# Block-sparse attention with a feed-forward layer: neighbour blocks of two tiles copied in v's own order, and conversions and keys moved

## The chip, the cores and the metric

The kernel runs on one core of a Trainium2 chip. The core has a matrix engine (TensorE, PE in the profile; its weight loads are PEld), a vector engine (VectorE, DVE), an activation engine (ScalarE, ACT), a general engine (GpSimd, POOL) and an engine that mainly issues DMAs (SyncE, SP). Each takes its own instructions in order; semaphores connect them. SBUF is the on-chip memory of 128 partitions, PSUM the accumulator memory that PE writes to. The metric is the device time of one execution in microseconds, as the median of several runs.

## The reference

Attention over a sparse set of blocks, then a feed-forward layer with a squared ReLU, all in float32. q, k and v are (4 batches, 8 heads, 768 positions, 64). Positions form 24 blocks of 32.

```python
mask = np.abs(blk_i - blk_j) <= window          # window = 1: a block and its two neighbours
mask = mask | (blk_i == 0) | (blk_j == 0) | (blk_i == n_blocks - 1) | (blk_j == n_blocks - 1)
for qb in range(n_blocks):
    for kb in sampled_blocks[qb]:               # 3 sampled blocks for each block of queries
        mask[qb * block:(qb + 1) * block, kb * block:(kb + 1) * block] = True
scores = np.where(mask, scores, -1000000000.0)
...
attn = attn / (np.sum(attn, axis=-1, keepdims=True) + 1e-09)
return np.matmul(attn, v)
...
h = np.maximum(x @ w_in, 0.0)                   # x: (3072, 512), w_in: (512, 2048)
return h * h @ w_out                            # w_out: (2048, 512)
```

So a block of queries sees eight blocks of keys: the first and the last of the sequence, three sampled ones and its own neighbourhood of three. The softmax doesn't depend on the order of these eight, as long as scores and values use the same one. The first and the last block of queries see all 24.

## The kernel before

**Tiles and stages.** The 768 positions of a batch are six tiles of 128 (four blocks each), 24 tiles in all, in the list `order`; index `k` counts them from 0. Three tiles (`UC`) make a chunk, whose 384 positions go through the feed-forward layer together. A stage of the program runs the feed-forward layer of one chunk (`moe(c)`) beside the attention of the next one. The start, before the first `moe(0)`, is the attention of tiles 0 to 2 alone, together with the first and last query blocks of batch 0 (`Whole`, four of them, tiles `g`, `pg`, `ptg`, `pTg`, `pvg` in the profile). Each tile's attention is two halves of four heads (`Half`): scores on PE (line 373, tile `s`), maxima on DVE (385), exponentials on ACT (432, `p`), transposes on PE (447, `pt`), their copies to SBUF on ACT (457, `pT`), products with the values on PE (471, `pv`), and the division by the sum on DVE (487 to 495).

**Order.** The order of each engine's instructions is written out by hand. A `Stream` counts steps (`now`). In the start a new unit begins every 5 steps, the wholes at 0 to 15 and the halves at 20 to 45, and each unit's next part comes so many steps later as `LAG_0` says (scores, +2 maxima, +2 exponentials, +3 transposes, +2 copies, +2 values, +2 norm). Between the steps the loop at line 951 hands out one copy from the list `fixed` to ACT (from step 7), one from `moves` to DVE (from step 22), one piece of the lists in `later` (keys) to POOL every second step, and one call of `cut_next` at each step that `CUT_0` names.

**Values of a tile.** A tile's eight blocks of values lie in two buffers, `V[k][0]` and `V[k][1]`, each of 128 partitions, that is four slots of 32, for two half-widths `i` and four query blocks `j`. `V[k][0]` holds the first and last block (slots 0, 1) and sampled blocks 0 and 1. `V[k][1]` holds sampled block 2 in slot 0 and the three neighbours in slots 1 to 3. For tiles 1 and 2 the neighbours aren't fetched from HBM: `copy_window` (211) copies each of them, 32 partitions by 260 elements, from `vn`, which has all of v of the batch with block b in partitions (b mod 4)·32 and column block b // 4. That is 12 copies for a tile and a half-width, 48 in all: 24 on ACT (`fixed`), 12 on POOL (ahead of the third tile's keys) and 12 on DVE (`moves`). The sampled blocks are fetched by SP (`load_sampled`, 303, issues on line 314), 65 KB each, with indices read into registers (`sampled`, 232).

**Keys of a tile.** `KG` holds first, last and sampled keys of a tile; POOL copies them from `kn` (`copy_keys`, 257; lines 267 and 288). The neighbours' keys are read straight from `kn`. So a half's scores are two pieces for each query block: one over three neighbouring blocks of `kn`, one over five blocks of `kg`. Keys of tiles 3 and 4 are appended to `later` as tiles 0 and 1 pass; two buffers alternate, so that tile 3 uses tile 0's, and tile 4 tile 1's.

**Weights.** The feed-forward weights come as 64-bit numbers and are converted to float32 by a pipeline that `cut_next` (768) pushes on by one: weight n is loaded by a DMA on POOL's queue (724), five calls later ACT does two operations (`cut`, 740 and 742), one call later DVE two (`cut_bits`, 751 and 752), one call later ACT and POOL split it where needed (758, 759). The order is four pieces of w_in, the first of w_out (`WO[0]`), and then both in turn. In `moe(0)` a call comes every 3 steps, and `need` (777) makes calls until a weight that is wanted has passed all stages. `moe(0)` runs over `f` from 0 to 15: `hidden` (line 820, `ph`; then ACT 824 and 827 make `gp`), and from f = 2 `project(f-2)` (line 848, `po`), which reads `gp` and `WO`. At f = 1 `split_wo` calls `need` for `WO[0]`. SINGLE pieces of w_in are split into two parts just ahead of their use (784 on ACT, 787 on POOL, `wi`).

Of the kernel before, what the change touches and what calls it, by code (L numbers as in the profile page):

```python
# [48 lines left out]
UC = 3  # L49
# [26 lines left out]
CUT_0 = (30, 5)  # L76
# [6 lines left out]
ON_ACT = 12  # L83
# [13 lines left out]
def tile_block_sparse_attention_moe(ctx: ExitStack, tc, kd, knd, qd, qgd, vd, vnd, samp, const, wcat, out):  # L97
# [113 lines left out]
    def copy_window(k, i, j, n, copy):  # L211

        b, t = order[k]
        blk = centre(NJ * t + j) - 1 + n
        assert 0 < blk < NBLK - 1
        r = blk % NJ * BLK
        copy(V[k][1][(1 + n) * BLK : (2 + n) * BLK, i, j], st["vn", b, i][r : r + BLK, blk // NJ])  # L217
# [85 lines left out]
    def load_sampled(k, u, eng, on):  # L303
        us = halves(k, u)
        if us is None:
            return
        b, t = order[k]
        VA, VB = values_of(k)
        vals = sampled(t, 1, on)
        v4 = columns(vd[b], us).rearrange("(a p) u c -> p a u c", p=BLK)  # L310
        for j in sorted(groups(t)):
            for r in range(NRAND):
                dst = VB[0:BLK, us, j] if r == 2 else VA[(2 + r) * BLK : (3 + r) * BLK, us, j]
                eng.dma_start(dst.unsqueeze(1), v4[:, bass.ds(vals[NRAND * j + r], 1)])  # L314
# [6 lines left out]
    class Half:  # L321
# [36 lines left out]
        def scores(self):  # L358
            b, t, u = self.b, self.t, self.u
            q, kg, kn = st["q", b, t], st["kg", b, t], st["kn", b, u]  # L360
            self.sb = [bank(f"s{self.name}_{e}") for e in range(2)]
            for i in range(2):
                pr = 2 * u + i
                for piece in range(2):
                    for g, j in enumerate(self.js):
                        c = centre(NJ * t + j)
                        for e in range(2):
                            r = slice(e * D, (e + 1) * D)
                            if piece == 0:
                                k, a, z = kn[r, c - 1 : c + 2, i, :], S_WIN, NSLOT  # L370
                            else:
                                k, a, z = kg[r, j, :, pr, :], 0, S_WIN
                            nc.tensor.matmul(  # L373
                                self.sb[e][g * BLK : (g + 1) * BLK, i * NSLOT + a : i * NSLOT + z],
                                q[r, j, pr, :],
                                k,
                                start=True,
                                stop=True,
                            )

# [535 lines left out]
    for k in range(1, UC):  # L916
# [11 lines left out]
    load_sampled(1, 0, nc.sync, SP)  # L928
    load_q(0, 2, own=begin)
    load_sampled(2, 1, nc.sync, SP)  # L930
    windows = {
        (k, u): [(copy_window, k, u, j, n) for j in range(NJ) for n in range(3)] for k in range(1, UC) for u in range(2)
    }
    for k in range(2):
        deque(copy_keys(0, k), 0)
    for _ in range(AHEAD):
        cut_next()
    for k in range(1, UC):
        if k == 1:
            for f, *at in windows[k, 0]:  # L940
                f(*at, nc.gpsimd.tensor_copy)
            deque(copy_keys(0, 2, begin), 0)
    fixed = [(copy_static, k, i) for k in range(UC) for i in range(2)]
    fixed += windows[2, 0] + windows[2, 1][:ON_ACT]
    moves = windows[1, 1] + windows[2, 1][ON_ACT:]
# [4 lines left out]
    now = 0  # L950
    while work.todo or work.running:
        work.step(now)
        now += 1
        if now % KEYS_N == 0 and later and next(later[0], True):
            later.pop(0)
# [3 lines left out]
        if now >= MOVES_0 and moves:  # L959
            f, *at = moves.pop(0)  # L960
            f(*at, nc.vector.tensor_copy)
        if now >= CUT_0[0] and (now - CUT_0[0]) % CUT_0[1] == 0:
            cut_next()
# [78 lines left out]
```

## Time and profile before

| what | us |
|---|---|
| median of 3 timed runs (lowest, highest) | 752.19 (750.61, 753.6) |
| the profiled execution: device time | 748.36 |
| its span, from the program's first instruction to its last | 746.6 |
| first `ph` matmul of `moe(0)` | 58.08 |

The profile page gives busy time by engine and by groups of instructions; `128x512 f32<-128x512 f32` is output and input in partitions by elements. Views by stretch and in order of time are read from the same execution, with times in us from the start of its span. A number in brackets with an arrow, as in `[0.49 <-PE pv L471]`, is how long the engine stood idle before an instruction, and what ended that. SPq is SP's queue, whose rows are the issues of DMAs, not their transfers.

### The profile page before, as it was taken

To read this page: it belongs to the slowest core of one execution; us is meant where nothing else is said; L and a number is where in the kernel's file an instruction comes from. 1 tells how busy PE (TensorE), PEld (TensorE's weight loads), DVE (VectorE), ACT (ScalarE), POOL (GpSimd) and SP (SyncE) were. 2 spreads that over 40 slices of the span, in tenths; PEclk is the share of its full clock that TensorE was granted. 3 is DMA by queue.
4 is the path that set the end of the run, shared out by engine and by line. 5 is a ranking of instruction groups with operands and counts; after the bars stand their busy time and mean duration, and the time that the engine had idled before them with its cause. 6 is when DMAs were issued, how large, how long until landed. Compare 5 with 4: busy or idle time off the path is not lost.

```text
span 746.6 us, 24386 instructions
## 1 busy us (share of the span) xinstructions
PE 717.3 (96%) x9000; PEld 596.6 (80%) x9000; DVE 509.1 (68%) x1052; ACT 518.5 (69%) x1145; POOL 497.0 (67%) x624
## 2 busy tenths in 40 slices
PE   4689999999999999999999999999999999999997
PEld 2566676668888888887888888887788888898996
DVE  5886886758885757667876665667878666555342
ACT  4996787888876866588786677578976776623222
POOL 6953644237876675767778567675777576877885
PEclk9999999999999999999999999999999999999999
DMA  8784889553533435543543445544344342101001
GB/s 274 227 234 144 242 258 338 134 151 78 144 93 91 139 92 162 151 106 91 143 86 99 120 99 158 162 98 129 84 128 107 90 126 54 34 1 43 0 2 43
DMA packets 85755, 92.44 MB, mean 124 GB/s; under 512 B 13539, under 2 KB 73444, under 8 KB 85636
## 3 DMA queue, kind: packets, MB, share of 16 engines
q1 hardware_dynamic: 79684, 68.03, 34.5%
q0 software_dynamic: 5664, 22.45, 9.0%
q8 instruction: 72, 1.18, 0.7%
q14 instruction: 47, 0.39, 0.2%
q10 hardware_dynamic: 288, 0.39, 0.1%
HBM read 84.53 MB, written 6.29 MB: 122 GB/s over the span
## 4 chain that ended last, share of the span: by engine, by line
PE 79%; ACT 8%; DMA 4%; DVE 3%; POOL 2%; issue 2%; SPq 1%; ACTq 0%; POOLq 0%; DVEq 0%
PE ph L820 32%; PE po L858 29%; PE s L373 6%; PE pv L471 5%; PE po L848 3%; DMA V<-in_v_dram 2%; ACT pm L418 2%; PE pvg L636 1%; ACT V L217 1%; DMA KG<-in_k_dram 1%; PE g L566 1%; PE xt L805 1%; ACT pg L591 1%; PE pt L447 1%; SPq L314 1%
## 5 line engine op out<-in xcount | busy, mean ns | idle before, releaser
L820 PE MATMUL ph<-xh,wi 128*128 128x384 f32 x832 | 238.1, 347 | 0.0
L418 ACT ACTIVATE pm<-p 32x256 f32<-32x256 f32 x528 | 219.1, 415 | 17.4 <-DVE p L393 9.9
L858 PE MATMUL po<-wo,gh 128*128 128x512 f32 x672 | 211.5, 396 | 0.0
L787 POOL TENSOR_TENSOR wi<-W,wi 128x512 fp32r<-128x512 f32 x104 | 142.8, 1373 | 71.3 <-DVE wi L786 37.5
L824 ACT ACTIVATE r<-ph 128x384 f32<-128x384 f32 x128 | 63.0, 493 | 167.9 <-PE ph L820 166.8
L787 POOL TENSOR_TENSOR wo<-WO,wo 128x512 fp32r<-128x512 f32 x112 | 144.7, 1292 | 50.1 <-DVE wo L786 42.1
L838 POOL TENSOR_TENSOR gl<-gf,gh 128x384 fp32r<-128x384 f32 x112 | 117.3, 1047 | 83.3 <-DVE gf L836 70.0
L820 PEld LDWEIGHTS ph<-xh,wi 128*128 128x128 f32 x832 | 150.6, 188 | 13.1 <-issue 6.2
L836 DVE SCALAR_TENSOR_TENSOR gf<-ph,r 128x384 f32<-128x384 f32 x112 | 62.3, 556 | 139.1 <-ACT r L824 119.4
L858 PEld LDWEIGHTS po<-wo,gh 128*128 128x128 f32 x672 | 122.8, 188 | 24.5 <-issue 5.8
L820 PE MATMUL ph<-xl,wi 128*128 128x384 f32 x416 | 141.2, 339 | 0.0
L858 PE MATMUL po<-wo,gl 128*128 128x512 f32 x336 | 132.6, 395 | 1.5 <-POOL gl L838 1.5
L820 PEld LDWEIGHTS ph<-xl,wi 128*128 128x128 f32 x416 | 78.1, 188 | 10.0 <-issue 6.5
L786 DVE CAST wo<-WO 128x512 fp32r<-128x512 f32 x112 | 83.4, 745 | 0.0
L858 PEld LDWEIGHTS po<-wo,gl 128*128 128x128 f32 x336 | 63.1, 188 | 16.8 <-POOL gl L838 3.3
L385 DVE TENSOR_REDUCE m<-s 128x2 f32<-128x512 f32 (+1 forms) x96 | 61.5, 681 | 7.2 <-PE s L373 6.8
L831 ACT ACTIVATE gh<-r 128x384 fp32r<-128x384 f32 x112 | 58.9, 526 | 9.4 <-POOL wo L787 0.4
L471 PEld LDWEIGHTS pv<-V,pT 128*32 128x32 f32 x2816 | 43.8, 109 | 21.7 <-issue 11.1
L471 PE MATMUL pv<-V,pT 128*32 128x65 f32 x2816 | 52.6, 221 | 6.8 <-ACT pT L457 5.1
L820 PE MATMUL ph<-xh,WI 128*128 128x384 f32 x192 | 54.1, 342 | 0.8 <-ACT xh L808 0.8
L373 PE MATMUL s<-KG,q 64*32 64x160 f32 x1408 | 48.8, 302 | 0.9 <-ACT KG L288 0.9
L393 DVE TENSOR_TENSOR p<-s,m 128x512 f32<-128x512 f32 (+1 forms) x72 | 46.0, 679 | 0.2
(90 smaller groups left out, 912.5 us busy)
## 6 DMA issues: line engine op xcount, KB each, us to landing
craw<-in_w_dram POOLq DMA_DIRECT2D x32, 512.0 KB, 6.3
V<-in_v_dram SPq DMA_DIRECT2D x462, 32.5 KB, 1.8
KG<-in_k_dram SPq DMA_DIRECT2D x198, 64.0 KB, 2.0
V<-in_v_dram SPq DMA_DIRECT2D x28, 390.0 KB, 4.2
q<-in_q_dram SPq DMA_DIRECT2D x24, 256.0 KB, 2.8
out_dram<-ot SPq DMA_DIRECT2D x22, 256.0 KB, 3.4
V<-in_v_dram SPq DMA_DIRECT2D x16, 292.5 KB, 4.8
vn<-in_vn_dram SPq DMA_DIRECT2D x5, 780.0 KB, 5.5
```

What stands on the lines that cost most here:

```text
L373: nc.tensor.matmul(self.sb[e][g * BLK : (g + 1) * BLK, i * NSLOT + a : i * NSLOT + z], q[r, j, pr, :], k, start=True, stop=True,)
L385: nc.vector.tensor_reduce(m[at, e], self.sb[e][at].rearrange("p (i c) -> p i c", i=2), axis=AX, op=ALU.max)
L418: nc.scalar.activation(p[a * BLK : (a + 1) * BLK, g], x[g * BLK : (g + 1) * BLK, :, a], AF.Exp, scale=SCALE)
L471: nc.tensor.matmul(po[g * BLK : (g + 1) * BLK, h * VW : (h + 1) * VW], self.pT[:, src, 2 * e + i, c], v[:, self.u, j, hv : hv + VW], start ...
L786: nc.vector.tensor_copy(w[:, 0], src)
L787: nc.gpsimd.tensor_tensor(w[:, 1], src, w[:, 0], op=ALU.subtract)
L820: nc.tensor.matmul(ph[:, :TOK], w, x, start=(i == 0), stop=(i == len(steps) - 1))
L824: nc.scalar.activation(r, ph[:, :TOK], AF.Relu)
L831: nc.scalar.activation(gh, r, AF.Square)
L836: nc.vector.scalar_tensor_tensor(gf, ph[:, :TOK], 0.0, r, op0=ALU.max, op1=ALU.mult)
L838: nc.gpsimd.tensor_tensor(gl, gf, gh, op=ALU.subtract)
L858: nc.tensor.matmul(acc[c][u], g[:, at], w[:, k], start=(f == 0 and i == 0), stop=(f == NF - 1 and i == 2))
```

## The change

For tiles 1 and 2 (`turned(k)`) the neighbour blocks keep the partitions that they have in `vn`: query block j has its own block in slot j of `V[k][1]`, the one before in slot j − 1 and the one after in slot j + 1, modulo 4. Sampled block 2 goes to the slot that is left, `free_place(j)`. One copy of 128 partitions fills all four query blocks with the tile's four blocks at once, and two copies of 32 partitions put in the last block of the tile before (for j = 0) and the first block of the tile after (for j = 3). The large copy also writes the free slot, so the sampled block 2 has to be fetched behind it. The scores' columns follow the new order of slots, for which the pieces of a query block become three (j = 1, and two for j = 2) or four (j = 0 and 3).

The three sets of copies of tile 1's two half-widths and of tile 2's first are on POOL, the last set on DVE; ACT has none. `CUT_0` becomes (36, 6). In the start's loop only the first list that enters `later` (tile 3's keys) is worked off; tile 4's goes on in `moe(0)`.

```diff
-CUT_0 = (30, 5)
+CUT_0 = (36, 6)
...
-ON_ACT = 12
...
-    def copy_window(k, i, j, n, copy):
+    def turned(k):
+        return 0 < k < UC
+    def free_place(j):
+        return (j + 2) % NJ
+    def copy_window(k, i, part, copy):
         b, t = order[k]
-        blk = centre(NJ * t + j) - 1 + n
-        assert 0 < blk < NBLK - 1
-        r = blk % NJ * BLK
-        copy(V[k][1][(1 + n) * BLK : (2 + n) * BLK, i, j], st["vn", b, i][r : r + BLK, blk // NJ])
+        dst, vn = V[k][1][:, i], st["vn", b, i]
+        if part == 0:
+            copy(dst, vn[:, t : t + 1].broadcast_to(list(dst.shape)))
+        elif part == 1:
+            copy(dst[P - BLK : P, 0], vn[P - BLK : P, t - 1])
+        else:
+            copy(dst[0:BLK, NJ - 1], vn[0:BLK, t + 1])
...
-    def load_sampled(k, u, eng, on):
+    def load_sampled(k, u, eng, on, rs=range(NRAND)):
...
-            for r in range(NRAND):
-                dst = VB[0:BLK, us, j] if r == 2 else VA[(2 + r) * BLK : (3 + r) * BLK, us, j]
+            for r in rs:
+                a = (free_place(j) if turned(k) else 0) * BLK
+                dst = VB[a : a + BLK, us, j] if r == 2 else VA[(2 + r) * BLK : (3 + r) * BLK, us, j]
...
-                for piece in range(2):
+                for piece in range(4 if turned(self.k) else 2):
...
-                            if piece == 0:
-                                k, a, z = kn[r, c - 1 : c + 2, i, :], S_WIN, NSLOT
-                            else:
-                                k, a, z = kg[r, j, :, pr, :], 0, S_WIN
+                            k, a = self.keys(piece, j, i, kn[r], kg[r, j, :, pr])
+                            if k is None:
+                                continue
+                            a = i * NSLOT + a * BLK
...
+        def keys(self, piece, j, i, kn, kg):
+            c = centre(NJ * self.t + j)
+            n, w = 2 + NRAND, S_WIN // BLK
+            if not turned(self.k):
+                return (kg, 0) if piece else (kn[:, c - 1 : c + 2, i], w)
+            f = 4 + free_place(j)
+            if piece == 0:
+                return (kg, 0) if f == n - 1 else (kg[:, : n - 1], 0)
+            first, last = (1 if j == 0 else 0), (2 if j == NJ - 1 else 3)
+            if piece == 1:
+                return kn[:, c - 1 + first : c - 1 + last, i], 4 + (j - 1 + first)
+            if piece == 2:
+                if first:
+                    return kn[:, c - 1 : c, i], 7
+                if last < 3:
+                    return kn[:, c + 1 : c + 2, i], 4
+                return (None, 0) if f == n - 1 else (kg[:, n - 1 :], f)
+            return (kg[:, n - 1 :], f) if j in (0, NJ - 1) else (None, 0)
...
-    load_sampled(1, 0, nc.sync, SP)
+    load_sampled(1, 0, nc.sync, SP, (0, 1))
+    windows = {(k, i): [(copy_window, k, i, n) for n in range(3)] for k in range(1, UC) for i in range(2)}
+    deque(copy_keys(0, 0), 0)
+    for i in range(2):
+        for f, *at in windows[1, i]:
+            f(*at, nc.gpsimd.tensor_copy)
+    deque(copy_keys(0, 1), 0)
     load_q(0, 2, own=begin)
-    load_sampled(2, 1, nc.sync, SP)
...
-    for k in range(2):
-        deque(copy_keys(0, k), 0)
+    load_sampled(1, 0, nc.sync, SP, (2,))
+    load_sampled(2, 1, nc.sync, SP, (0, 1))
     for _ in range(AHEAD):
         cut_next()
-    for k in range(1, UC):
-        if k == 1:
-            for f, *at in windows[k, 0]:
-                f(*at, nc.gpsimd.tensor_copy)
-            deque(copy_keys(0, 2, begin), 0)
+    for f, *at in windows[2, 0]:
+        f(*at, nc.gpsimd.tensor_copy)
+    deque(copy_keys(0, 2, begin), 0)
     fixed = [(copy_static, k, i) for k in range(UC) for i in range(2)]
-    fixed += windows[2, 0] + windows[2, 1][:ON_ACT]
-    moves = windows[1, 1] + windows[2, 1][ON_ACT:]
+    moves = windows[2, 1]
...
-        if now % KEYS_N == 0 and later and next(later[0], True):
+        ahead = ahead or (later[0] if later else None)
+        if now % KEYS_N == 0 and later and later[0] is ahead and next(ahead, True):
...
             f(*at, nc.vector.tensor_copy)
+            if not moves:
+                load_sampled(2, 1, nc.sync, SP, (2,))
```

More of the change, by code (lines that the diff above doesn't have):

```diff
@@ L363, in scores @@
                 pr = 2 * u + i
-                for piece in range(2):
+                for piece in range(4 if turned(self.k) else 2):
                     for g, j in enumerate(self.js):
-                        c = centre(NJ * t + j)
                         for e in range(2):
                             r = slice(e * D, (e + 1) * D)
-                            if piece == 0:
-                                k, a, z = kn[r, c - 1 : c + 2, i, :], S_WIN, NSLOT
-                            else:
-                                k, a, z = kg[r, j, :, pr, :], 0, S_WIN
+                            k, a = self.keys(piece, j, i, kn[r], kg[r, j, :, pr])
+                            if k is None:
+                                continue
+                            a = i * NSLOT + a * BLK
                             nc.tensor.matmul(
-                                self.sb[e][g * BLK : (g + 1) * BLK, i * NSLOT + a : i * NSLOT + z],
+                                self.sb[e][g * BLK : (g + 1) * BLK, a : a + k.shape[1] * BLK],
                                 q[r, j, pr, :],
@@ L927, in tile_block_sparse_attention_moe @@
     load_sampled(0, 0, nc.sync, SP)
-    load_sampled(1, 0, nc.sync, SP)
-    load_q(0, 2, own=begin)
-    load_sampled(2, 1, nc.sync, SP)
-    windows = {
-        (k, u): [(copy_window, k, u, j, n) for j in range(NJ) for n in range(3)] for k in range(1, UC) for u in range(2)
-    }
-    for k in range(2):
-        deque(copy_keys(0, k), 0)
+    load_sampled(1, 0, nc.sync, SP, (0, 1))
[5 more added lines that the diff above has]
+    deque(copy_keys(0, 1), 0)
+    load_q(0, 2, own=begin)
+    load_sampled(1, 0, nc.sync, SP, (2,))
+    load_sampled(2, 1, nc.sync, SP, (0, 1))
     for _ in range(AHEAD):
         cut_next()
-    for k in range(1, UC):
-        if k == 1:
-            for f, *at in windows[k, 0]:
-                f(*at, nc.gpsimd.tensor_copy)
-            deque(copy_keys(0, 2, begin), 0)
+    for f, *at in windows[2, 0]:
+        f(*at, nc.gpsimd.tensor_copy)
+    deque(copy_keys(0, 2, begin), 0)
     fixed = [(copy_static, k, i) for k in range(UC) for i in range(2)]
-    fixed += windows[2, 0] + windows[2, 1][:ON_ACT]
-    moves = windows[1, 1] + windows[2, 1][ON_ACT:]
+    moves = windows[2, 1]
     side = lambda name: ps_o.tile([P, 512], F32, tag="o", name=name)
@@ L950, in tile_block_sparse_attention_moe @@
     now = 0
+    ahead = None
     while work.todo or work.running:
```

## The prediction

> **What bounds the kernel now.** I read the page first, then busy time by stretches, then the groups of lines of the first 62 us, then the engines one by one in order of time. The page, its first line and PE's busy tenths in 40 slices:
>
> ```profile
> span 746.6 us, 24386 instructions
> PE   4689999999999999999999999999999999999997
> ```
>
> PE is full in every slice but the first three and the last. The change touches that start: the attention of tiles 0 to 2, before the first `ph`. Stretches around it (length, busy time of PE, PEld, DVE, ACT, POOL, granted clock, DMA share, GB/s):
>
> ```profile
> 20.00:30.00 10.00, 8.21 (x236) 6.69 (x237) 8.31 (x25) 9.74 (x24) 9.44 (x28) 1.00 1.00 320
> 30.00:40.00 10.00, 6.34 (x213) 4.99 (x192) 9.37 (x28) 9.75 (x23) 10.00 (x44) 0.94 0.69 169
> 40.00:50.00 10.00, 8.34 (x273) 6.48 (x273) 9.52 (x24) 9.70 (x21) 3.96 (x12) 0.89 0.74 194
> 60.00:70.00 10.00, 10.00 (x110) 8.21 (x88) 5.97 (x9) 6.31 (x13) 2.41 (x3) 1.00 0.34 95
> ```
>
> From 20 to 50 us ACT is full (9.7 of 10) and DVE nearly so, while PE has room. From 60 on PE is full and ACT has room. So the time is the moment of the first `ph` plus PE's work from there. A microsecond won before that moment is worth one at the end, unless PE then waits for something that used to be ready.
>
> ```profile
> 28.53 0.93 PE L447 MATMUL pt<-ident,p 96*128 96x96 f32 x8
> 52.20 1.09 PE L447 MATMUL pt<-ident,p 128*128 128x128 f32 x8
> 58.08 0.44 PE L820 MATMUL ph<-xh,WI 128*128 128x384 f32 x1 [0.78 <-ACT xh L808]
> ```
>
> I measure the start by the transposes `pt` of the six halves (three tiles, two halves each): the first and the last are 23.7 us apart, five steps, and 5.9 us later comes `ph`.
>
> **The change part by part.** *Copies of neighbour blocks.* From the groups by line (count, busy us, mean ns, idle before):
>
> ```profile
> L217 ACT COPY V<-vn 32x260 f32<-32x260 f32 x24 | 9.7, 405 | 0.4
> L217 POOL COPY V<-vn 32x260 f32<-32x260 f32 x12 | 4.8, 398 | 0.5
> L217 DVE COPY V<-vn 32x260 f32<-32x260 f32 x12 | 4.4, 363 | 0.3
> L288 POOL COPY KG<-kn 128x512 f32<-128x512 f32 x6 | 3.7, 615 | 5.6 <-DMA kn<-in_kn_dram 5.5
> ```
>
> All 48 go. Four sets are added, each one copy of 128x1040 and two of 32x260: three sets on POOL, one on DVE. The large copy is in no row of these engines. On POOL 260 elements take 0.398 and 512 take 0.615, that is 0.86 ns an element, so 1.07; with two small ones at 0.44 (4.8 + 0.5 over 12) a set is 1.95. On DVE the ends are one small copy, 0.36, and four, 1.45; I take 1.1, near the four, and 1.8 for the set. ACT loses 9.7 us of work, DVE 2.6.
>
> *Conversions.* `CUT_0` goes from six calls (steps 30, 35, ... 55) to four (36, 42, 48, 54), so two conversions leave the start. Rows of one on ACT and what follows it, and the end of one on DVE:
>
> ```profile
> 44.24 0.70 ACT L740 ACTIVATE W<-craw 128x512 f32<-128x512 f32 x1
> ...
> 45.46 0.64 ACT L758 CAST WI<-ct 128x512 fp32r<-128x512 f32 x1
> 51.13 0.69 DVE L752 SCALAR_TENSOR_TENSOR W<-craw,W 128x512 int32<-128x512 int32 x1
> ```
>
> One is two operations on ACT, 1.22 from start to the next start (45.46 − 44.24); I use 1.3, and twice 0.69 on DVE. Two are 2.6 and 2.8.
>
> *POOL.* Two sets, 3.9 us, now stand ahead of the second tile's keys; these ended at 19.25, where the weight loads begin, and will end at 23.1. The loads (2.62) and the third set follow, so the third tile's keys start at 27.7 for 27.2:
>
> ```profile
> 19.25 2.62 POOL L724 DMA_DIRECT2D craw<-in_w_dram  x5
> 27.20 0.61 POOL L288 COPY KG<-kn 128x512 f32<-128x512 f32 x1
> ```
>
> That is hidden: their first reader, tile 2's scores, comes behind 35 us even by the steps below. The fifth tile's keys move behind the first `ph`, where POOL is busy 2.41 of 10. I count nothing.
>
> *Scores.* A turned half issues 13 pieces where there were 8, over the same columns: 104 records for 64. PE's rows at full clock, from the chain of work:
>
> ```profile
> 70.25 1.14 PE s L373 x63
> 68.68 0.87 PE pt L447 x8
> 75.56 1.41 PE pv L471 x64
> ```
>
> By columns scores stay at 1.14, by records they take 1.85. I take 1.5, the middle, on four halves.
>
> *The new steps.* ACT per half, and the copies ahead of `pTg` that go:
>
> ```profile
> 18.69 0.82 ACT L217 COPY V<-vn 32x260 f32<-32x260 f32 x2
> 50.20 1.07 ACT L457 COPY pT<-pt 128x512 f32<-128x512 f32 x2 [0.44 <-PE pt L447]
> 51.16 1.59 ACT L432 ACTIVATE p<-s,m 128x256 f32<-128x256 f32 x4
> ```
>
> By starts 0.96 and, less overlap, 1.5. With a conversion ACT needs 3.8 a half, and PE as much: 1.5 + 1.41 + 0.87. Two steps come before the first conversion and are PE's: 1.5 of scores, 1.06 of `pv` (48 of 64 records), 0.93 of transposes, 3.5 each. Two have a conversion, 3.8 each. The last also has the `WI` cast, about 0.5 more: 4.3. Together 18.9 for 23.7, **4.8 earlier**.
>
> The first transposes win only 0.3: DVE's work leads up to them. It starts 0.8 earlier, without ACT's two copies at 18.69, but the set of 1.8 takes the place of three small copies, 0.39 + 0.53 + 0.41, in this list:
>
> ```profile
> 21.14 0.16 DVE L647 TENSOR_SCALAR recg<-pvg 128x1 f32<-128x1 f32 x1 [1.36 <-PE pvg L636]
> 22.94 0.39 DVE L217 COPY V<-vn 32x260 f32<-32x260 f32 x1
> 25.00 0.53 DVE L217 COPY V<-vn 32x260 f32<-32x260 f32 x1
> 26.88 0.41 DVE L217 COPY V<-vn 32x260 f32<-32x260 f32 x1
> ```
>
> *SP and the data.* The blocks of slot 2 are now fetched behind the copies that would overwrite them. Rows of SP's issues, the landing of tile 2's last load, all landings of V:
>
> ```profile
> 6.65 22.20 SPq L314 DMA_DIRECT2D V<-in_v_dram  x21
> 29.38 0.35 SPq L246 DMA_DIRECT2D q<-in_q_dram  x1
> 31.19 9.85 SPq L314 DMA_DIRECT2D V<-in_v_dram  x12
> V<-in_v_dram SPq DMA_DIRECT2D x1, 65.0 KB, 4.0
> DMA to landing us min/median/max: 1.7/5.4/11.3
> ```
>
> The loads are the same 33, ending at 41.05; added are two reads of the block indices. One stands between 29.73 and 31.19, 1.46 with its waits; at 1.0 and without the waits around that query the end is 42.2, with everything 44.0. I take 42.9, the last issue 0.7 earlier, landed at 46.2. The copies are done by 27.7 and aren't waited for. Tile 2's first `pv` has to start 1.4 before the last transposes (28.2 + 18.9 = 47.1), at 45.7. So **0.5 is lost**; between nothing and 2.5 (44.0 − 0.7 + 5.4 = 48.7, 3.0 late, of which 0.5 is counted).
>
> Start: 4.8 + 0.3 − 0.5 = **4.6 earlier**. Its upper end is DVE's work, almost without a gap from 21.14 to 51.8: 2.6 + 2.8 less, begun 0.8 earlier, 6.2. The lower is 2.1, with the data at 48.7.
>
> *The clock.* Two stretches:
>
> ```profile
> 35.00:38.00 3.00, 0.49 (x17) 0.15 (x6) 2.78 (x10) 2.92 (x7) 3.00 (x13) 1.00 0.57 122
> 38.00:42.60 4.60, 4.53 (x119) 3.70 (x120) 4.34 (x13) 4.49 (x11) 2.14 (x9) 0.63 0.94 275
> ```
>
> PE idles from 35 to 38, and then its clock is 0.63 for 4.6 us. The new steps have no such gap, so I count them at full clock. [...]
>
> *The later stage.* The two missing calls come back when `need` asks for WO[0] at f=1. So WO[0] is cut only after `hidden(0)`. Before, another weight is converted in just that place, and its rows price it:
>
> ```profile
> 62.61 0.49 ACT L824 ACTIVATE r<-ph 128x384 f32<-128x384 f32 x1 [4.06 <-PE ph L820]
> 63.62 0.65 ACT L740 ACTIVATE ct<-craw 128x512 f32<-128x512 f32 x1
> 64.52 2.74 PE L848 MATMUL po<-WO,gp 128*128 128x512 f32 x6
> 64.95 0.69 DVE L751 SCALAR_TENSOR_TENSOR ct<-ct,craw 128x512 int32<-128x512 int32 x1 [1.17 <-ACT craw L742]
> 65.68 1.64 DVE L752 SCALAR_TENSOR_TENSOR ct<-craw,ct 128x512 int32<-128x512 int32 x1
> ```
>
> The first `po`, at 64.52, reads WO[0]; a weight converted in that slot is ready at 67.32. **PE waits 2.7**, counting 0.1 for its overlap with the last `ph`; 1.8 if the second DVE operation takes 0.69 as at 51.13. Behind the wait stand `hidden(2)` and all PE's work. ACT's 2.6 more fit where it is busy 6.31 of 10.
>
> **Sum:** 746.6 − 4.6 + 2.7 = 744.7 of span. The profiled execution took 748.36 around its 746.6; the three timed runs have a median of 752.19, 3.8 above it. On that scale 752.2 − 1.9 = **750.3**.
>
> **The rivals.** *A, faster:* the start reaches DVE's 6.2 and PE waits 1.8: 4.4 won, 747.8. For it: ACT loses more work (12.3) than the start can gain. Against it: PE and ACT need 3.8 a half whatever DVE does. *B, slower:* tile 2's last blocks land late, because the weight loads of 512 KB begin 3.9 us later, into the fetching of these blocks. Each microsecond beyond 46.2 costs one; from 48.1 on the kernel is slower than before. With the longest landing, 11.3 behind 42.2, it is 53.5: 7.3 lost, 757.6; at 50, 754.1. Against it: the weight loads should be through by 37. *C:* WO[0] is ready in time and PE doesn't wait: 747.6. Against it stands the order of conversions. That the copies stay can't be; their lines are replaced.
>
> **How the numbers follow.** Forecast (0 to 3.8 won) 0.6, A 0.16, C 0.08, B 0.16, of which 0.07 beyond half a per cent (landing behind 52). Half a per cent is 3.8 us, about what a measurement of this kernel can tell from no change; A and C lie just over it. Faster 0.24, same 0.69, slower 0.07. The range runs from 746.8 (A with C's missing wait in part) to 754.1 (B at 50).
>
> **What would show it.** No 32x260 copies on ACT; `ph` first at 53.5; a `po` with some 2.7 of idle time before it, ended by DVE's WO; 104 records in a turned half's scores; clock 1.00 from 38 to 43. `ph` behind 56, or `pv` waiting for V by more than 2, breaks the first term; a `po` without a wait the last.

## The result and the profile after

| | before | after |
|---|---|---|
| median of 6 timed runs each, same chip (lowest, highest) | 750.85 (749.67, 753.6) | 758.55 (758.4, 760.52) |
| profiled execution, its span | 748.36, 746.6 | 758.43, 756.3 |
| first `ph` | 58.08 | 62.57 |
| from the first `ph` to the end of the span | 688.5 | 693.7 |

The changed kernel takes **1.0103** times as long, 95% interval 1.0082 to 1.0123. The forecast was 750.3 with a range of 746.8 to 754.1, so it was wrong, on the side to which it gave 0.07. The span grew by 9.7: 4.5 ahead of the first `ph`, 5.2 behind it.

First TensorE's timeline of the changed kernel: start, length, engine, line, operation, number; in brackets the idle time before and its releaser. A record is one matmul of the trace.

```profile
29.19 0.88 PE L477 MATMUL pt<-ident,p 96*128 96x96 f32 x8
...
33.32 0.49 PE L383 MATMUL s<-KG,q 64*32 64x128 f32 x16
...
33.89 0.45 PE L383 MATMUL s<-KG,q 64*32 64x32 f32 x10
37.76 0.49 PE L383 MATMUL s<-KG,q 64*32 64x128 f32 x6 [3.42 <-issue]
...
43.01 1.11 PE L501 MATMUL pv<-V,pT 128*32 128x65 f32 x44
46.69 0.54 PE L501 MATMUL pv<-V,pT 128*32 128x65 f32 x20 [2.56 <-issue]
...
51.16 0.26 PE L383 MATMUL s<-KG,q 64*32 64x32 f32 x5 [0.30 <-issue]
...
56.06 1.53 PE L501 MATMUL pv<-V,pT 128*32 128x65 f32 x64 [2.58 <-ACT p L462]
57.52 1.09 PE L477 MATMUL pt<-ident,p 128*128 128x128 f32 x8
...
62.57 0.44 PE L850 MATMUL ph<-xh,WI 128*128 128x384 f32 x1 [0.82 <-ACT xh L838]
...
71.94 2.90 PE L878 MATMUL po<-WO,gp 128*128 128x512 f32 x3 [2.79 <-DVE WO L782]
```

The `po` at 71.94 waits as forecast. In the three rows with `<-issue` TensorE stands still in the middle of a run of equal matmuls, after 56 of the 104 records of one half's scores, after 44 of the 64 of one half's products, and nothing that the profile shows releases it. The kernel before has two such rows, one of 0.39 at 43.91 and this one:

```profile
48.76 0.76 PE L471 MATMUL pv<-V,pT 128*32 128x65 f32 x36 [1.22 <-issue]
```

The windows view of the changed kernel between its pauses counts what was executed:

```profile
31.29:37.76 6.47, 3.05 (x130) 2.54 (x126) 3.11 (x10) 4.37 (x11) 6.47 (x36) 0.97 0.91 260
37.76:46.69 8.93, 6.37 (x253) 5.72 (x254) 5.94 (x15) 3.74 (x8) 2.19 (x9) 0.83 0.78 211
46.69:51.16 4.47, 4.17 (x128) 3.62 (x128) 0.77 (x3) 3.02 (x7) 0.00 (x0) 0.62 0.49 129
...
70.00:80.00 10.00, 8.06 (x84) 5.52 (x90) 5.74 (x8) 6.56 (x14) 4.47 (x13) 0.83 0.67 207
```

Matmuls (second number in brackets after PE busy) and weight loads together are 256, 507 and 256; with seven waits that are instructions of their own, and the edges counted once, the second is 512. The DMA queues on the two pages, packets and MB, say what comes in such portions; first before, then after:

```profile
PE 717.3 (96%) x9000; PEld 596.6 (80%) x9000; DVE 509.1 (68%) x1052; ACT 518.5 (69%) x1145; POOL 497.0 (67%) x624
...
q8 instruction: 72, 1.18, 0.7%
```

```profile
PE 722.6 (96%) x9160; PEld 602.0 (80%) x9160; DVE 506.3 (67%) x1043; ACT 508.1 (67%) x1121; POOL 495.6 (66%) x621
...
q8 instruction: 73, 1.20, 0.7%
```

73 packets of 16.4 KB for the 18,733 instructions that the trace has of TensorE (waits included), and 72 for the 18,409 of before, are one packet for every 256, 64 bytes of it for each; so I take it that queue q8 brings TensorE's instructions. The DMA view of the changed kernel from 34.9 to 36.4 has one such packet, and that from 36.4 to 37.7 has none:

```profile
q8 instruction: 1, 0.02, 5.4%
```

5.4% of 16 engines in 1.5 us are 1.3 us. By its record it ran from 35.00 to 36.30, and TensorE went on at 37.76. In the traces of both kernels every such pause up to 80 us ends 1.3 to 1.6 after such a packet (1.2 to 1.7 in those of all the runs below), at an instruction whose number, counted through TensorE's instructions in the trace, is 193 or 194 more than a multiple of 256. **Theory 1** is therefore that the start of the changed kernel is limited by the fetching of TensorE's instructions: a half has 272 before and 352 after. Rivals: POOL's copies of 128 partitions slow DVE (theory 2); sampled blocks of V come too late, since SP loads the last of them behind the copies (theory 3); the two moved conversions are the cause by themselves.

### The profile page after: what moved, and what is told of

Same layout as the page of the kernel before. It is cut to its first block, busy times and chain, and to the rows that moved or that the text cites. A ratio compares the mean times of both kernels' runs of the same rounds, so it can differ in the third digit from the quotient of the medians.

```text
span 756.3 us, 24680 instructions
## 1 busy us (share of the span) xinstructions
PE 722.6 (96%) x9160; PEld 602.0 (80%) x9160; DVE 506.3 (67%) x1043; ACT 508.1 (67%) x1121; POOL 495.6 (66%) x621
## 4 chain that ended last, share of the span: by engine, by line
PE 81%; ACT 7%; DVE 7%; issue 2%; POOL 2%; DMA 1%; ACTq 0%; DVEq 0%; POOLq 0%
PE ph L850 32%; PE po L888 28%; PE s L383 7%; PE pv L501 6%; PE po L878 4%; ACT pm L448 1%; PE pvg L666 1%; PE g L596 1%; PE pt L477 1%; DVE m L415 1%; PE xt L835 1%; ACT craw L772 1%; ACT r L854 1%; DMA kn<-in_kn_dram 1%; DVE WO L782 1%
## 5 line engine op out<-in xcount | busy, mean ns | idle before, releaser
L383 PE MATMUL s<-KG,q 64*32 64x160 f32 (+2 forms) x1504 | 51.9, 298 | 4.7 <-issue 3.7
L878 PE MATMUL po<-WO,gp 128*128 128x512 f32 x96 | 46.3, 618 | 2.8 <-DVE WO L782 2.8
```

The lines of the kernel that those rows point to most:

```text
L383: nc.tensor.matmul(self.sb[e][g * BLK : (g + 1) * BLK, a : a + k.shape[1] * BLK], q[r, j, pr, :], k, start=True, stop=True,)
L878: nc.tensor.matmul(acc[c][u], g[:, u * P : (u + 1) * P], WO[f], start=(f == 0), stop=(f == NF - 1))
```

## The experiments

Ratios are to the kernel before on the same chip; first `ph` and the time behind it are from the one profiled execution of each, which took the longest of all its runs in e1, e3, e7, e8, e14 and e15, and the shortest in e4 and e11. That column moves from one execution to the next: ahead of the first `ph` e5 has the same instructions as e2, and e11 the same as the changed kernel, and their first `ph` are 58.06 and 56.48, 63.10 and 62.57. A difference of up to 1.6 in it shows nothing by itself. e2, e5, e6, e9 and e12 give other scores than the reference's; they show times and are no kernels to use.

| run | ratio (95% interval) | first `ph` | behind it |
|---|---|---|---|
| e1 conversions back in the start | 1.0058 (1.0032, 1.0083) | 64.75 | 688.2 |
| e2 two pieces | 1.0040 (1.0025, 1.0055) | 56.48 | 691.6 |
| e3 before, 13 pieces | 1.0039 (1.0025, 1.0053) | 59.79 | 693.2 |
| e4 wide scores | 1.0119 (1.0088, 1.0149) | 59.15 | 692.9 |
| e5 e2, WO[0] asked for early | 1.0005 (0.9985, 1.0025) | 58.06 | 690.5 |
| e6 before, 40 records | 0.9995 (0.9980, 1.0011) | 58.25 | 690.4 |
| e7 weight loads first | 1.0067 (1.0041, 1.0093) | 62.25 | 693.3 |
| e8 wide, several edits | 1.0048 (1.0023, 1.0072) | 64.12 | 692.0 |
| e9 40 records, WO[0] early | 0.9999 (0.9983, 1.0015) | 53.23 | 693.6 |
| e10 wide, queries by ACT | 1.0078 (1.0052, 1.0104) | 63.31 | 691.4 |
| e11 WO[0] early alone | 1.0103 (1.0082, 1.0125) | 63.10 | 690.3 |
| e12 40 records, conversions back | 0.9980 (0.9960, 1.0000) | 57.02 | 689.5 |
| e13 wide, conversions back | 1.0069 (1.0044, 1.0095) | 64.11 | 690.2 |
| e14 wide, conversions late | 1.0090 (1.0060, 1.0120) | 62.67 | 695.5 |
| e15 stream shifted | 1.0116 (1.0084, 1.0149) | 63.26 | 693.8 |
| e16 before, conversions late | 1.0033 (1.0013, 1.0054) | 58.38 | 693.0 |

**The pieces: e2 takes them out of the change, e3 puts them alone into the kernel before.** In e2 the scores are again one piece over `kn` and one over `kg`:

```diff
-                for piece in range(4 if turned(self.k) else 2):
+                for piece in range(2):
...
-            if not turned(self.k):
+            if True:
                 return (kg, 0) if piece else (kn[:, c - 1 : c + 2, i], w)
```

> The changed kernel with the scores of tiles two and three in two pieces for each block, as before the change: 64 records a half for 104. The slots of the scores then aren't those of the values, so these two tiles' output is other than the reference's; the amount of all other work is unchanged. Theory 1 (instruction fetch): 160 matmuls and 160 weight loads fewer, the pauses without a releaser in the middle of scores shrink, first ph at 55 to 58 against 62.57, po still waits 2.5 to 3, time 751 to 754. Theory 2 (POOL's large copies slow DVE) and theory 3 (sampled blocks land later): first ph stays at 62 to 63, time 757 to 760.

In e3 the kernel before cuts the same pieces for tiles 1 and 2 (4, 3, 2 and 4 of them for the four blocks):

```diff
+                        if 0 < self.k < UC:
+                            n = (4, 3, 2, 4)[j]
+                            parts = [(kg[:, j, 0 : 5 if n == 2 else 4, pr, :], 0)]
...
```

> The kernel before with one thing of the change: the scores of tiles two and three in 13 pieces for each pair of a half, of the same lengths as the change's, for 8; slots, copies, loads and conversions as before. Theory 1 (instruction fetch): the 160 matmuls and 160 weight loads that come on top meet the same limit, first ph at 61 to 64 against 58.08, pauses without a releaser every 256 instructions of TensorE, time 754 to 758. Theories 2 and 3 and the moved conversions: nothing of theirs is in it; it is as before or up to 1 later for the plain time of 40 more records a half, time 750 to 752.

TensorE's timeline of e2, then of e3, then e3's windows:

```profile
37.09 0.43 PE L501 MATMUL pv<-V,pT 128*32 128x65 f32 x16 [2.84 <-issue]
46.61 0.76 PE L501 MATMUL pv<-V,pT 128*32 128x65 f32 x36 [1.69 <-issue]
...
56.48 0.44 PE L850 MATMUL ph<-xh,WI 128*128 128x384 f32 x1 [0.82 <-ACT xh L838]
```

```profile
32.84 0.19 PE L385 MATMUL s<-KG,q 64*32 64x32 f32 x1 [2.25 <-issue]
36.84 0.34 PE L385 MATMUL s<-KG,q 64*32 64x128 f32 x6 [0.95 <-issue]
41.98 0.28 PE L385 MATMUL s<-kn,q 64*32 64x96 f32 x7 [1.51 <-issue]
45.75 0.53 PE L483 MATMUL pv<-V,pT 128*32 128x65 f32 x19 [1.69 <-issue]
49.67 0.25 PE L385 MATMUL s<-KG,q 64*32 64x32 f32 x4 [0.97 <-issue]
...
63.88 0.50 PE L385 MATMUL s<-KG,q 64*32 64x160 f32 x5 [1.79 <-issue]
```

```profile
62.00:66.00 4.00, 2.21 (x47) 1.63 (x44) 0.46 (x1) 0.00 (x0) 0.00 (x0) 0.60 0.20 43
66.00:70.00 4.00, 4.00 (x15) 4.00 (x14) 2.29 (x5) 1.52 (x4) 0.57 (x1) 0.55 0.00 0
```

Without the pieces the changed start is 6.1 shorter (5.0 between e5 and e11), with nothing else altered; with them alone the kernel before is 0.39% slower and gets a pause at every block of 256. The reorderings of theories 2 and 3 are all in e2 and none is in e3: they fall as the main cause. The size in e3 was overestimated (754 to 758 expected, 751.68 measured, which lies in the rivals' 750 to 752). Its start lost only 1.7, no more than the plain time of the added records (four halves at 1.54 for 1.14 are 1.6 by the rows of the changed kernel and of before), though its pauses up to 49.67 are 7.4 in sum: where TensorE has to wait for ACT and DVE anyway, most of a pause costs nothing. Another 1.8 comes with a pause behind the first `ph`, in the longest of its ten runs, and the clock falls after that, to means of 0.60 and 0.55 in the two windows above. So e3 shows the pauses, and e2 what they cost beside a start with less work on ACT and DVE.

**The position: e15.** Tile one's halves compute the window's scores twice, so that the stream behind them is shifted by 96 instructions:

```diff
-                for piece in range(4 if turned(self.k) else 2):
+                for piece in range(4) if turned(self.k) else (0, 0, 1) if self.k == 0 else (0, 1):
```

> The changed kernel, in which tile one's two halves compute the scores of their windows twice over (the second time into the same place, so the output stays): 48 matmuls and 48 weight loads more on TensorE ahead of everything that follows, nothing else moved. Theory 1 (the pauses are blocks of 256 instructions being fetched): the pauses stay at the same count of instructions and so fall 96 instructions earlier in the program. The first long one, which stood after 56 of the 104 records of the second tile's second half, falls after 8 of them; first ph at 61 to 65. Rival (the pauses belong to the instructions they stand before, a wait for data that the trace doesn't name): they stay at those instructions, after 56 of 104.

```profile
33.35 0.88 PE L477 MATMUL pt<-ident,p 96*128 96x96 f32 x8
34.16 0.42 PE L383 MATMUL s<-KG,q 64*32 64x128 f32 x8
37.23 0.33 PE L383 MATMUL s<-KG,q 64*32 64x160 f32 x4 [2.65 <-issue]
```

The pause now stands after 8 of the 104 records, where it stood after 56: it belongs to the place in the stream, not to the instruction.

**The weight loads: e7.** The five calls of `cut_next` ahead of the loop stand before the second tile's window copies:

```diff
+    for _ in range(AHEAD):
+        cut_next()
     for i in range(2):
         for f, *at in windows[1, i]:
...
-    for _ in range(AHEAD):
-        cut_next()
```

> The changed kernel with POOL's five weight loads of 512 KB issued ahead of the second tile's window copies, at some 17 us, in place of behind the second tile's keys, at 24.13; nothing else. Theory 1a (the fetch waits in the DMA engines behind these loads): the loads have landed by 31, the fetch for instruction 961 begins under 2 after the one before is used up in place of 3.7, and the pause of 3.42 at 37.76 falls below 1.5; first ph at 60 to 61.5, time 755 to 757. Theory 1b (the turnaround is 4 to 6 us whatever moves on the DMA): pause 2.5 to 3.5 as changed, first ph at 62 to 63.5, time 758 to 760, since the second tile's keys also come 2.6 later.

```profile
35.27 0.34 PE L383 MATMUL s<-KG,q 64*32 64x128 f32 x6 [0.92 <-issue]
39.29 0.28 PE L383 MATMUL s<-kn,q 64*32 64x96 f32 x7 [0.86 <-issue]
45.07 0.86 PE L501 MATMUL pv<-V,pT 128*32 128x65 f32 x20 [3.58 <-issue]
```

The pause of 3.42 falls to 0.92, as 1a had it (the packet starts 1.8 after the block before was entered, where it was 3.7): here the fetch took less when these loads were not on the DMA. The other traces fit that: in the changed kernel and the eleven others that issue these loads in the same place, this packet starts between 34.5 and 35.7, though the block before was entered anywhere from 30.2 to 33.2; it starts within 0.6 of the landing of the fourth of the five loads in the eleven traces that have this landing (in the changed kernel at 35.00, for 34.99). In e7 all five have landed by 28.81, and the packet starts at 32.95. But the 2.5 that TensorE is ahead by then are given back from 45.07 on, where the packet begins 3.1 after the block before was entered, and where the granted clock is 0.50 from 44.38 to 54.62. So the time of 755.66 is in 1a's range, and first `ph` at 62.25 in 1b's.

**The conversions.** e1 puts them back into the changed start (`CUT_0 = (30, 5)`), e16 moves only them in the kernel before (`CUT_0 = (36, 6)`). e11 and e5 ask for WO[0] ahead of `hidden(0)`, in the changed kernel and in e2:

```diff
+            if c == 0 and f == 0:
+                need(0, 1)
             yield from hidden(c, f)
```

> The changed kernel with CUT_0 = (30, 5) again, so that the two conversions return to the start; the copies, the slots and the pieces stay as changed. Theory 1 (TensorE stands still for want of instructions in the start; the later conversions cost what the wait of 2.79 before the first po and the lower clock of 70 to 80 us show): first ph stays near 62.6 or comes up to 1 later, the wait before po goes to below 0.5, clock of 70 to 80 above 0.95, span 751 to 753 against 756.3, time 753 to 756. Rival (the moved conversions are the main cause): first ph near 58, time 749 to 751. Rival (late data or POOL beside DVE): first ph as changed, 62 to 63, like theory 1.

> The kernel before with CUT_0 = (36, 6): of the change only that two conversions leave the start. If ACT and DVE limit the start of before (as the prediction had it, and e6 leaves), two conversions less bring its first ph 2 to 4 earlier, to 54 to 56.5; the wait for WO[0] and in part the clock cost 2.5 to 5 behind it: time 749 to 752.5, level with before or up to 0.4% slower. If the start of before has another limit: first ph at 57.5 to 58.5 and time 752 to 755.

> The changed kernel with WO[0] asked for ahead of hidden(0), nothing else. If the late conversion costs its wait and the clock behind it: first ph at 61.5 to 63.5, no idle time over 0.3 before the first po, the clock of 70 to 80 above 0.95 for 0.83, time 753 to 755.5, 3.5 to 5 below the changed kernel. Rival (only the wait, the clock falls at the next pause of instruction fetch all the same): time 755.5 to 757. Second rival (the wait moves to ph): no gain, 757.5 to 760.

> As e2 (changed kernel, scores of tiles two and three in two pieces, so that these tiles' output is other than the reference's), and WO[0] is asked for ahead of hidden(0) in place of after it. Theory 1 (instruction fetch in the start, and the conversion that the first po waits for, are the two costs): first ph at 55 to 58 as in e2, no idle time over 0.3 before the first po, clock of 70 to 80 us back above 0.95, time 745 to 748, 3 to 5 below e2 and 1 to 4 below the kernel before of the same chip. Rival (the wait only moves, since ACT and DVE have no room beside hidden(0)): a wait of 1.5 to 3 before ph or po stays, time 750 to 752.

Timelines of e16, e11 and e5 in turn:

```profile
48.15 0.88 PE L471 MATMUL pv<-V,pT 128*32 128x65 f32 x36 [2.53 <-issue]
...
58.38 0.44 PE L820 MATMUL ph<-xh,WI 128*128 128x384 f32 x1 [0.78 <-ACT xh L808]
...
67.76 4.10 PE L848 MATMUL po<-WO,gp 128*128 128x512 f32 x6 [2.79 <-DVE WO L752]
```

```profile
75.29 0.62 PE L850 MATMUL ph<-xh,wi 128*128 128x384 f32 x2 [2.68 <-POOL wi L817]
```

```profile
70.25 0.61 PE L850 MATMUL ph<-xh,wi 128*128 128x384 f32 x2 [2.65 <-POOL wi L817]
```

e1 gives the time behind the first `ph` back (688.2), and loses 2.2 ahead of it, where up to 1 was expected. With the conversions back the changed kernel still is 0.58% slower than before: by themselves they aren't the cause. e16 has 4.5 more behind the first `ph` and nothing in return: in its one profiled start a pause of 2.53, and a clock of 0.50 behind it (eight `pt` took 1.97 at 48.96, and 1.09 at 52.62), take what ACT and DVE were spared. Its first `ph` is as the second expectation has it, its time (751.69) as the first. Asking early doesn't remove the wait, it moves it from `po` to the next `ph`: the conversions of the start that are missing have to be done somewhere between 60 and 75, and TensorE waits 2.7 for them either way. In e11 the ratio doesn't move, as its second rival has it, though its time of 757.12 lies just under that rival's range. Its profiled execution, the shortest of four, kept the clock at 1.00 behind the wait and has 690.3 behind the first `ph`; the median of the four doesn't show that gain. In e5 the rival was right (a wait stays, 750.40); e5 is 0.35% below e2, with intervals that touch, and what gives it that isn't settled.

**Both limits at once: e6, e9, e12.** Three of the four blocks of tiles 1 and 2 take their scores from one matmul over eight neighbouring key blocks (as many columns, 40 records a half); e6 does this in the kernel before, e9 in the changed one with WO[0] asked for early, e12 in the changed one with `CUT_0 = (30, 5)`:

```diff
+            if turned(self.k) and j < NJ - 1:
+                return (None, 0) if piece else (kn[:, c - 1 : c + 7, i], 0)
```

> The kernel before, where the first three blocks of tiles two and three get their scores in one matmul of eight neighbouring key blocks in place of two matmuls: as many columns, 40 records a half for 64, 96 matmuls and 96 weight loads fewer. These blocks' scores are then other ones than the reference's; the work of all other engines is the same. Theory 1 (the start is limited by the fetching of TensorE's instructions already before the change): first ph at 54 to 56.5 against 58.08, time 745 to 747.5 where the kernel before has 748.8. Rival (ACT and DVE limit the start of before, as the prediction had it): first ph at 57.5 to 58.5, time 748 to 749.5.

> The changed kernel with e6's scores (the first three blocks of tiles two and three in one matmul each, 40 records a half in place of 104, other scores than the reference's) and WO[0] asked for ahead of hidden(0) as in e5. Theory 1 in the form that e6 leaves (two limits stand close together: ACT and DVE, which the change relieves, and the fetching of TensorE's instructions, which it loads): with both relieved the start goes to what the prediction had, first ph at 53 to 55.5, time 743.5 to 746.5. Rival (the blocks of V that SP loads, one each 0.75 us, or POOL's keys set the pace of the new steps): pv waits for V or s for keys, first ph at 56.5 to 58.5, time 747 to 750.5.

> As e9 (changed kernel, scores of tiles two and three in 40 records a half, other scores than the reference's), but with CUT_0 = (30, 5), so that the two conversions are in the start, and WO[0] is asked for where the changed kernel asks for it. Theory 1 (fetching held the changed start; two missing conversions cost some 2.5 later wherever they are asked for): first ph at 54.5 to 56.5, no wait of the first po or second ph above 0.5, the time behind the first ph back to 688 to 689, time 744.5 to 747, below the kernel before by 2.5 or more. Rival (the two conversions cost the start as much as they cost later): first ph at 57 to 58.5, time 747.5 to 750.

Timelines of e9 and of e12:

```profile
28.89 1.54 PE L479 MATMUL pt<-ident,p 96*128 96x96 f32 x8
...
48.09 1.09 PE L479 MATMUL pt<-ident,p 128*128 128x128 f32 x8
...
53.23 0.45 PE L852 MATMUL ph<-xh,WI 128*128 128x384 f32 x1 [0.82 <-ACT xh L840]
...
63.55 0.44 PE L852 MATMUL ph<-xh,wi 128*128 128x384 f32 x1 [1.17 <-ACT wi L816]
65.39 0.62 PE L852 MATMUL ph<-xh,wi 128*128 128x384 f32 x2 [1.22 <-POOL wi L819]
```

```profile
43.19 0.46 PE L383 MATMUL s<-KG,q 64*32 64x160 f32 x4 [1.72 <-issue]
...
50.52 0.43 PE L503 MATMUL pv<-V,pT 128*32 128x65 f32 x16 [1.56 <-issue]
...
57.02 0.45 PE L852 MATMUL ph<-xh,WI 128*128 128x384 f32 x1 [0.82 <-ACT xh L840]
```

e9, at 749.35, is in its rival's range by the time, but it reaches the forecast start, with fewer records than the forecast counts: first `ph` at 53.23 (53.5 forecast), five steps from 28.89 to 48.09, 19.2 (18.9 forecast). Theories 2 and 3 can't cost much then, since POOL's copies and SP's order are those of the change. In e6 fewer instructions bring nothing (its start still has pauses of 1.90 and 0.98), and from 28.53 to 52.20 of the kernel before ACT is busy 22.87 of 23.67 and DVE 22.08: the start of before has ACT and DVE as a limit as well. So **two limits lay side by side**, and the change relieves one while it loads the other. But e9's time is that of before, since 5.1 are lost behind the first `ph`; and with the conversions back (e12, 749.34) 3.8 of the start are lost again, partly to two pauses: its rival was right, the conversions cost the start what they cost later. The most that was seen of the idea is e12's 0.2%, with an interval that ends at no change, and e12 leaves out scores that the reference has.

**Wider matmuls: e4, e8, e10, e13, e14.** One matmul of 128 queries against the tile's own four key blocks takes the place of the pieces over `kn`; the places that belong to the neighbours and to sampled block 2 are overwritten: 9 pieces, 72 records.

```diff
+                if turned(self.k):
+                    for e in range(2):
+                        r = slice(e * D, (e + 1) * D)
+                        nc.tensor.matmul(
+                            self.sb[e][:, i * NSLOT + 4 * BLK : (i + 1) * NSLOT],
+                            q[r, :, pr, :].rearrange("k a c -> k (a c)"),
+                            kn[r, NJ * t : NJ * (t + 1), i, :],
...
```

For this the queries of a tile have to lie pair by pair, and are loaded in four parts in runs of 128 bytes.

> The changed kernel with the window's scores of all four blocks of tiles two and three in one matmul (128 queries against the tile's four own key blocks; the two neighbours and the third sampled block then overwrite the places that are theirs): 9 pieces for 13, 72 records a half for 104. The fourth block's neighbour sits one place higher, and the queries of these two tiles are loaded by pair, in runs of 128 bytes. Theory 1 (instruction fetch): first ph at 56 to 59, po still waits 2.5 to 3, time 752 to 755; if the queries in short runs land late, up to 3 more. Theories 2 and 3: first ph at 62 to 63, time 757 to 760.

> A version that computes all of the reference: the changed kernel with e4's wide scores (72 records a half), the weight loads first as in e7, all six window copies on POOL ahead of the third tile's keys (so that DVE has none and the third tile's last sampled blocks are loaded some 15 us earlier), and WO[0] asked for ahead of hidden(0). If the causes found so far are all: first ph at 55 to 57.5, no wait of pv for V over 0.3, none of po, time 745 to 748 against 748.8 of the kernel before. If the queries in runs of 128 bytes or the later keys hold tile two back: first ph at 58 to 61, time 749 to 752.

> Computes all of the reference: e4's wide scores (72 records a half), WO[0] asked for ahead of hidden(0), and the queries of tiles two and three, in four parts each, loaded from ACT's queue early in place of SP's, so that SP's loads of V aren't behind them as in e4 (there tile three's last one was issued at 50.33, for 42.74 in the changed kernel). Theory 1: first ph at 55 to 58, no wait of pv for V above 0.5, time 745 to 749. If V is late again (by SP's pace or by the DMA engines, busy with short runs at the beginning): first ph at 59 to 62, time 751 to 755.

> Computes all of the reference: the changed kernel with e4's wide scores (72 records a half), tile three's queries loaded in four parts from ACT's queue at some 24 us in place of SP's (tile two's in four parts from SP's), and CUT_0 = (30, 5). Theory 1: V of tile three in time, pauses of instruction fetch below 1.5 in sum, first ph at 57 to 59.5, the time behind it 688 to 689.5, time 747 to 750, level with the kernel before. Rival (DMA in short runs, or ACT standing still for its queue, costs as much as fetching did): first ph at 60 to 63, time 751 to 754.

> As e13, with the changed kernel's CUT_0 = (36, 6). Theory 1: first ph 1 to 2.5 earlier than in e13, at 55.5 to 58, then 2.5 to 5 more behind it (the wait for WO[0] and the clock): time 749 to 752, above e13's. If the start has room for the conversions: e13 lower by 2.5 or more; if not: both within 1.5 of each other.

SP's queue in the changed kernel and in e4, then TensorE in e8, then ACT in e13:

```profile
25.76 0.59 SPq L256 DMA_DIRECT2D q<-in_q_dram  x1
27.41 15.90 SPq L325 DMA_DIRECT2D V<-in_v_dram  x16
```

```profile
29.75 3.92 SPq L260 DMA_DIRECT2D q<-in_q_dram  x4
34.77 16.12 SPq L331 DMA_DIRECT2D V<-in_v_dram  x16
```

```profile
52.90 0.42 PE L511 MATMUL pv<-V,pT 128*32 128x65 f32 x2 [2.19 <-DMA V<-in_v_dram]
55.48 0.43 PE L511 MATMUL pv<-V,pT 128*32 128x65 f32 x2 [2.16 <-DMA V<-in_v_dram]
```

```profile
17.84 4.68 ACTq L260 DMA_DIRECT2D q<-in_q_dram  x4
22.56 0.58 ACT L663 COPY pTg<-ptg 128x512 f32<-128x512 f32 x1 [3.97 <-DMA V<-in_v_dram]
```

In e4 the third tile's 16 loads of V begin 7.4 later than in the changed kernel, and in e8 TensorE waits for them, 8 times and 7.0 in sum: there SP's order sets the pace. From ACT's queue four such loads hold ACT itself for 4.7 in e13 and 3.5 in e10 (the idle time that the next row of e13 puts down to V's landing is those issues), and everything behind comes later. None of the five beats the kernel before, and e8, e10, e13 and e14 (753.48, 755.64, 756.44 and 758.63) came out above every range expected of them; how much of that is the loads and how much the pauses, which e10, e13 and e14 still have, wasn't taken apart. That a layout of q in HBM with the pairs apart would help wasn't tried.

## Why the prediction was wrong

- **The step that failed** is "The new steps": it put 18.9 for five of them, 104 records a half taken at TensorE's own pace of 1.5. They took 28.3 (`pt` from 29.19 to 57.52). The pace was right: the first of the four halves runs its 104 records from 30.00 to 31.54. What was missing is that the instructions have to be there: 160 matmuls bring 160 weight loads, a half is 352 instructions for 272, and where TensorE had to wait, a block of 256 took 4.5 to 6.5 us to come round (2.0 to 3.7 until its packet starts, 0.9 to 1.4 for it, 1.3 to 1.5 until TensorE goes on). Of the 9.4 too many, 6.3 are the length of the three pauses, and some 3.1 the clock, which is 0.50 from 37.41 to 40.82 and from 47.65 to 51.06, with 3.06 and 3.21 us of TensorE's work in these stretches. That is a sum of lengths: the experiments price the pieces (e2), not each pause, and the last of the five steps also holds a wait of 2.58 for ACT. The trace of before has such a pause too, 1.22 ahead of 48.76, without a releaser; the prediction didn't ask what it was.
- **That TensorE has room** was read from its busy share in before, 6.34 of 10 from 30 to 40 and 8.34 from 40 to 50. The share didn't show the instructions' supply: in the second of these stretches stand the pauses of 0.39 and 1.22 that nothing in the trace releases.
- **What bounded before**: ACT and DVE did (e6), as stated; but fetching was next to them (e16's pause of 2.53 came with two conversions less), and was not named. How close it was isn't measured.
- **The start's other terms** are off by less and in part cancel. The first transposes came at 29.19 for 28.2 (at 28.78 to 29.66 in e1, e2, e5, e7, e9, e11, e12 and e15). DVE's list ahead of them, which was to start 0.8 earlier, started at 21.49 for 21.14. Beside POOL's copies (the second large one ran from 16.24 to 17.28) two of DVE's operations at 15.77 took 1.54, where they took 0.44 at 15.72 in before, which fits a little of theory 2; whether that is all of it isn't shown. The 0.5 for late data wasn't lost, and the way from the last transposes to `ph` took 5.1 for 5.9. With the steps that is 9.4 + 1.0 − 0.5 − 0.8, the 9.1 between 53.5 and 62.57. That e9 comes so close to 53.5 is in part luck of the same kind (0.3 + 0.7 − 0.5 − 0.7). POOL's large copy took 1.05 (1.07 estimated), DVE's 0.82 (1.1).
- **Late data, rival B**: V of the third tile landed at 46.75, 0.55 later than forecast, and TensorE didn't wait for it, since its own steps came later still. In e8 TensorE did wait for such blocks, 7.0 in sum.
- **WO[0]**: the wait was 2.79 for 2.7, the best term of the sum, and for the reason given: DVE's second operation again took long, 1.65. Rival C is out. What it lacked is the slower clock that came with it here, next point.
- **The clock** was counted at full. Between 20 and 750 us the changed kernel's trace has it at 1.00 but for three stretches of 3.41 us at 0.50, from 37.41, 47.65 and 71.54; the 0.83 and 0.62 of the windows are means of the two. The third has 3.01 us of TensorE's work in it, so 1.5 is lost, which with the wait makes up most of the 5.2 lost behind the first `ph`. The row from before had a clock of 0.63 behind 3 us with 0.49 of work in them; the wait of 2.7 that I added myself was not held against it. The three stretches stand beside idle times of 3.42 (up to 37.76), 2.56 (up to 46.69) and 2.79 (up to 71.94): the first begins 0.35 ahead of the end of its idle time, the second 0.96 behind it, the third 0.40 ahead. Beside the 2.58 up to 56.06 there is none.
- **Rival A** needed a start faster still. No rival had the supply of instructions in it, so the range of the unknown costs ended where the known engines did.

The parts by ratio: the pieces alone 0.39% (e3), the conversions alone 0.33% (e16), all but the pieces 0.40% (e2), all 1.03%. They don't add up exactly; what the rest is was not taken apart.

## What to carry to other kernels

Where TensorE's instructions are short, count them per stage: here a packet came for every 256 of them, weight loads too (73 for 18,733), and the signs were idle times `<-issue` in the middle of equal matmuls, a block or more apart (3.42 ahead of 37.76, 2.56 ahead of 46.69). Splitting matmuls to save copies on other engines bought their time with this one's (e2: without the pieces the start is 6.1 shorter). Work that is pushed out of a stage has to be free where it lands (two conversions cost a wait of 2.79 here), and a second limit just under the first left a relief nothing (e6, 0.9995; e16, 1.0033).

## What was not expected of the hardware

- In all these traces a pause in the instruction supply ended 1.2 to 1.7 us after the packet, which took 0.9 to 1.5; where TensorE paused, the packet had started 1.1 to 6.8 us after the block before it was entered (2.0 to 3.7 in the two kernels). That time is the part that varied: in e7, where the five weight loads had landed before, it was 1.8 for 3.7. The longest pause was 3.73, ahead of 53.15 in e1.
- Between 20 and 740 us the clock is 0.50 or 1.00 in all these traces, and 0.50 for 3.41 us (once in before, from 38.80; three times in the changed kernel) or two or three times that (6.83 in e3, 10.24 in e7 from 44.38). It was 0.50 from 62.76 to 69.59 in e3, beginning in a pause of 1.79, from 66.36 to 69.78 in e9 after waits of 1.17 and 1.22, and not at all in e5, where the windows from 66 to 82 show 1.00 behind a wait of 2.65. What decides it stays open.
- Four loads of 64 KB in runs of 128 bytes held the issuing queue for 3.9 us on SP (e4) and 3.5 to 4.7 us on ACT (e10, e13), against 0.59 for the same 256 KB in one piece.
